# Splitting sliding-window attention into a projection phase and a core phase that runs between the steps of SSM kernel generation

## The chip, the cores and the metric

The kernel runs on one core of a Trainium2 chip. The metric is the device time of one execution in microseconds (us). Before the change the median of 15 runs was 621.43 us (620.1 to 622.94). The spread of one kernel's runs is a few us, so a difference of 3 us in a single trace is not read as an effect.

PE is the matmul engine, PEld its weight loads, DVE the vector engine, ACT the scalar engine, POOL GpSimd, SP the sync engine, which here only issues DMAs. ACTq and SPq mark DMA issues on an engine's queue.

## The reference, cut to what matters

```python
g = sigmoid((x * gate_w).sum(-1, keepdims=True))
a = attention(x)          # 32 heads of 20; each position sees 8 positions, 2 apart
b = ssm(x)                # long convolution
return g * a + (1 - g) * b

# attention: qkv = x @ wqkv ; logits = q . k[gathered] ; softmax over 8 ; sum with v ; @ wo
# ssm:       K[d, l] = Re sum_n C B dt exp(dt A l)     (192 states, 2048 steps)
#            y = irfft(rfft(x, 4096) * rfft(K, 4096)) + x * Dskip
```

S is 2048 and D is 640. Attention and the SSM kernel K do not depend on each other. Only the last line joins them.

## The kernel before

It has three stages, one after the other.

1. Attention in four blocks of 512 positions, projection and core together. The arithmetic that turns the SSM parameters into the operand tables `Sprm` is cut into steps, and `hook()` puts some steps between the parts of attention.
2. Generation of K in ten chunks. A chunk builds its arguments by matmul (`ar`), takes sines (`qtr`, `ptr`) and exponentials (`e0`, `e1`) on ACT, multiplies them on DVE (`qr`, `qi`, `pt`), and contracts them on PE into `kps`. The first FFT step of each chunk goes straight into `bufA` in SBUF.
3. The FFT convolution: the spectrum of x (`Bu`), the products with the kernel's spectrum (`Y`), the inverse (`bufA`, then `bp`), and the gated sum (`tt`, `ot`).

```python
# 1. core of attention, per block of SC = 512 positions (cut)
for e in range(5):
    prod = wk.tile([128, W, SC], BF16, name="prod")
    nc.vector.tensor_tensor(prod[:], q_broadcast, k_window, ALU.mult)
    # ... 32 matmuls into lg
hook()
# ... softmax on DVE, one Exp on ACT; attention weights spread to asb on PE and ACT
for e in range(5):
    pv = wkb.tile([128, W, SC], BF16, name="pv")
    nc.vector.tensor_tensor(pv[:], win(vc[:, e, :], 0, W, DIL, SC), asb[:], ALU.mult)
    op = ps.tile([128, SC], F32, name="op")
    for w in range(W):
        nc.tensor.matmul(op[:], ident[:], pv[:, w, :], start=(w == 0), stop=(w == W - 1))
    nc.scalar.activation(oT[:, e, :], op[:], ACT.Identity)

# 2. generation (cut)
for c in range(NCH):
    L = kg.load_L(c)                                       # 8 small DMAs from Sprm
    kps = pk.tile([128, 2, 512], F32, name="kps")
    def fin(c=c, kps=kps):
        kc = kk.tile([128, 8, 64, 2], BF16, name="kc")
        nc.vector.tensor_copy(kc[:], ...)
        fft_f1(nc, pk, ..., F1c, Bk, c, ...)               # Bk is a view of bufA
    kg.chunk(c, L, pa, kps, fin)

# 3. between the two halves of the convolution (cut)
nc.scalar.dma_start(PSI[:], ...)
for g in range(4):
    (nc.sync if g % 2 == 0 else nc.scalar).dma_start(gaF[...], ...)
    nc.sync.dma_start(omF[...], omS...)                    # omS: 1 - g, two bf16 per position
```

Of the kernel before, what the change touches and what calls it, by code (L numbers as in the profile page):

```python
# [51 lines left out]
class Attn:  # L52

    def __init__(self, ctx, tc, x, wqkv, wo, gate_w, ga_sb, omg_sb):
        self.tc, self.nc = tc, tc.nc
        nc = tc.nc
        self.x, self.ga, self.omg = x, ga_sb, omg_sb
        ind_np, ident_np, sel_np, mask0_np = _attn_consts()
        cst = ctx.enter_context(tc.tile_pool(name="at_cst", bufs=1))
        self.cst = cst  # L60
        self.wq_sb = cst.tile([128, NKT, 3 * D], BF16, name="wq_sb")
        self.xT = cst.tile([128, NKT, S], BF16, name="xT")
        self.ident = cst.tile([128, 128], BF16, name="ident")
        nc.scalar.dma_start(self.ident[:], nc.inline_tensor(ident_np, name="c_ident").ap())
        wr = wqkv.rearrange("(k p) c -> p k c", p=128)
        for kt in range(NKT):
            nc.scalar.dma_start(self.wq_sb[:, kt], wr[:, kt])
        self.ind = cst.tile([128, 32], BF16, name="ind")
        nc.scalar.dma_start(self.ind[:], nc.inline_tensor(ind_np, name="c_ind").ap())
        self.sel = cst.tile([128, 4, 128], BF16, name="sel")  # L70
        nc.scalar.dma_start(self.sel[:], nc.inline_tensor(sel_np, name="c_sel").ap())
        self.mask0 = cst.tile([128, W, 32], F32, name="mask0")
        nc.scalar.dma_start(self.mask0[:], nc.inline_tensor(mask0_np, name="c_mask0").ap())
        self.gw_sb = cst.tile([128, NKT], BF16, name="gw_sb")
        nc.scalar.dma_start(self.gw_sb[:], gate_w.rearrange("(k p) -> p k", p=128))
        self.wo_sb = cst.tile([128, 5, D], BF16, name="wo_sb")
        nc.scalar.dma_start(self.wo_sb[:], wo.rearrange("(p e) c -> p e c", e=5))
        self.g_sb = cst.tile([128, 16], F32, name="g_sb")

    def prologue(self, ctx):  # L80
        tc, nc = self.tc, self.nc
        self.wk = wk = ctx.enter_context(tc.tile_pool(name="at_wk", bufs=2))
        self.ps = ps = ctx.enter_context(tc.tile_pool(name="at_ps", bufs=2, space=PSUM))
        xT, ident = self.xT, self.ident
        xnp = tc.tile_pool(name="at_xn", bufs=1)
        xpool = xnp.__enter__()
        xn = xpool.tile([128, 16, D], BF16, name="xn")
        xr = self.x.rearrange("(i p) d -> p i d", p=128)
        for sc in range(NSC):
            nc.sync.dma_start(xn[:, 4 * sc:4 * sc + 4], xr[:, 4 * sc:4 * sc + 4])  # L90
        for sc in range(NSC):
            c0 = sc * SC
            for kt in range(NKT):
                tx = ps.tile([128, SC], F32, name="pj")
                for i in range(4):
                    nc.tensor.matmul(tx[:, i * 128:(i + 1) * 128], xn[:, 4 * sc + i, kt * 128:(kt + 1) * 128], ident[:], start=True, stop=True)
                nc.scalar.activation(xT[:, kt, c0:c0 + SC], tx[:], ACT.Identity)
            gz = ps.tile([128, SC], F32, name="pj")
            for i in range(4):
                for kt in range(NKT):  # L100
                    nc.tensor.matmul(gz[:, i:i + 1], xT[:, kt, c0 + i * 128:c0 + (i + 1) * 128], self.gw_sb[:, kt:kt + 1], start=(kt == 0), stop=(kt == NKT - 1))
            ge = wk.tile([128, 4], F32, name="ge")
            nc.scalar.activation(ge[:], gz[:, 0:4], ACT.Exp, scale=-1.0)
            nc.vector.tensor_scalar(ge[:], ge[:], 1.0, None, ALU.add)
            gs = self.g_sb[:, 4 * sc:4 * sc + 4]
            nc.vector.reciprocal(gs, ge[:])
            nc.vector.tensor_scalar(self.omg[:, 4 * sc:4 * sc + 4], gs, -1.0, 1.0, ALU.mult, ALU.add)
        xnp.__exit__(None, None, None)

    def run(self, ctx, hook=lambda: None, gaS=None):  # L110
        tc, nc = self.tc, self.nc
        wk, ps = self.wk, self.ps
        wkb = ctx.enter_context(tc.tile_pool(name="at_wkb", bufs=2))
        xT, wq_sb, ind, ident, sel = self.xT, self.wq_sb, self.ind, self.ident, self.sel
        scale = float(DH) ** -0.5
        kprev = vprev = None
        for sc in range(NSC):
            c0 = sc * SC
            qc = wk.tile([128, 5, SC], BF16, name="qc")
            kc = wk.tile([128, 5, HALO + SC], BF16, name="kc")  # L120
            vc = wk.tile([128, 5, HALO + SC], BF16, name="vc")
            if sc == 0:
                nc.vector.memset(kc[:, :, 0:HALO], 0.0)
                nc.vector.memset(vc[:, :, 0:HALO], 0.0)
            else:
                nc.vector.tensor_copy(kc[:, :, 0:HALO], kprev[:, :, SC:SC + HALO])
                nc.vector.tensor_copy(vc[:, :, 0:HALO], vprev[:, :, SC:SC + HALO])
            kprev, vprev = kc, vc
            for which, dst, off in ((0, qc, 0), (1, kc, HALO), (2, vc, HALO)):
                for e in range(5):  # L130
# [4 lines left out]
                    nc.scalar.activation(dst[:, e, off: off + SC], pp[:], ACT.Identity)  # L135
            lg = ps.tile([128, 4, W, 32], F32, name="lg", bufs=1)
            for e in range(5):
                prod = wk.tile([128, W, SC], BF16, name="prod")
                nc.vector.tensor_tensor(prod[:], qc[:, e, :].unsqueeze(1).to_broadcast([128, W, SC]), win(kc[:, e, :], 0, W, DIL, SC), ALU.mult)  # L139
                for i in range(4):  # L140
                    for w in range(W):
                        nc.tensor.matmul(lg[:, i, w, :], prod[:, w, i * 128:(i + 1) * 128], ind[:],  # L142
                                         start=(e == 0 and w == 0 and i % 2 == 0), stop=(e == 4), skip_group_check=True)
            hook()
            lgs = wk.tile([128, 4, W, 32], F32, name="lgs")
            if sc == 0:
                nc.vector.tensor_tensor(lgs[:, 0], lg[:, 0], self.mask0[:], ALU.add)
# [3 lines left out]
            mx = wk.tile([128, 4, 32], F32, name="mx")  # L151
            nc.vector.tensor_reduce(mx[:], lgs[:].rearrange("p i w h -> p i h w"), AX.X, ALU.max)
            nc.vector.tensor_tensor(lgs[:], lgs[:], mx[:].unsqueeze(2).to_broadcast([128, 4, W, 32]), ALU.subtract)
            nc.scalar.activation(lgs[:], lgs[:], ACT.Exp, scale=scale)
            sm = wk.tile([128, 4, 32], F32, name="sm")
            nc.vector.tensor_reduce(sm[:], lgs[:].rearrange("p i w h -> p i h w"), AX.X, ALU.add)
            rs = wk.tile([128, 4, 32], F32, name="rs")
            nc.vector.reciprocal(rs[:], sm[:])
            at = wkb.tile([128, 4, W, 32], BF16, name="at")
            nc.vector.tensor_tensor(at[:], lgs[:], rs[:].unsqueeze(2).to_broadcast([128, 4, W, 32]), ALU.mult)  # L160
            atT = wkb.tile([128, 2, SC], BF16, name="atT")
            for wg in range(2):
                tp = ps.tile([128, SC], F32, name="tb")
                for i in range(4):
                    nc.tensor.matmul(tp[:, i * 128:(i + 1) * 128], at[:, i, 4 * wg:4 * wg + 4, :].rearrange("p w h -> p (w h)"), ident[:], start=True, stop=True)
                nc.scalar.activation(atT[:, wg, :], tp[:], ACT.Identity)
            asb = wkb.tile([128, W, SC], BF16, name="asb", bufs=1)
            for w in range(W):
                ab = ps.tile([128, SC], F32, name="tb")
                nc.tensor.matmul(ab[:], sel[:, w % 4, :], atT[:, w // 4, :], start=True, stop=True)  # L170
                nc.scalar.activation(asb[:, w, :], ab[:], ACT.Identity)  # L171
            hook()
            oT = wkb.tile([128, 5, SC], BF16, name="oT", bufs=1)
            for e in range(5):
                pv = wkb.tile([128, W, SC], BF16, name="pv")
                nc.vector.tensor_tensor(pv[:], win(vc[:, e, :], 0, W, DIL, SC), asb[:], ALU.mult)  # L176
                op = ps.tile([128, SC], F32, name="op")
                for w in range(W):
                    nc.tensor.matmul(op[:], ident[:], pv[:, w, :], start=(w == 0), stop=(w == W - 1))  # L179
                nc.scalar.activation(oT[:, e, :], op[:], ACT.Identity)  # L180
            hook()
            for i in range(4):
                it = sc * 4 + i
                for hf in range(2):
                    ap_ = ps.tile([128, SC], F32, name="op")
                    for e in range(5):
                        nc.tensor.matmul(ap_[:, :320], oT[:, e, i * 128:(i + 1) * 128], self.wo_sb[:, e, hf * 320:(hf + 1) * 320], start=(e == 0), stop=(e == 4))
                    nc.scalar.activation(self.ga[:, it, hf * 320:(hf + 1) * 320], ap_[:, :320], ACT.Identity, scale=self.g_sb[:, it:it + 1])  # L188
            if gaS is not None:
# [515 lines left out]
```

## Time and profile before

| stage | ends at (us) | length (us) |
|---|---|---|
| 1, until the first sine eviction `qtr` on ACT | 258.0 | 258.0 |
| 2, until the last `kps` matmul | 487.1 | 229.0 |
| 3, until the end | 620.8 | 133.7 |

The next lines are the busy time by stretch of the kernel before. Behind each stretch stand its length, then for each engine the busy us and, in brackets, the number of instructions. The last three columns are PE's mean granted clock (1.00 is full), the mean busy share of the DMA engines, and GB/s.

```profile
core 0: us, PE busy (x) PEld busy (x) DVE busy (x) ACT busy (x) POOL busy (x), PEclk, DMA share, GB/s
180.00:240.00 60.00, 38.95 (x227) 18.00 (x231) 40.13 (x25) 22.01 (x38) 0.00 (x0) 0.71 0.32 63
300.00:360.00 60.00, 51.57 (x1217) 26.15 (x1219) 40.42 (x54) 58.24 (x68) 8.39 (x6) 0.50 0.08 18
...
0.00:256.00 256.00, 183.63 (x1465) 101.89 (x1484) 170.39 (x131) 122.32 (x204) 3.87 (x7) 0.89 0.24 64
261.00:486.00 225.00, 179.93 (x4026) 92.20 (x4028) 152.56 (x207) 214.42 (x249) 22.60 (x16) 0.50 0.06 14
487.00:621.00 134.00, 88.59 (x1096) 58.37 (x1088) 78.59 (x75) 61.39 (x44) 0.00 (x0) 0.79 0.37 96
```

Stage 1 leaves every engine idle for long: in its last part ACT works 22 of 60 us. Stage 2 is held by ACT, which works 58.24 of 60 us, while DVE has a third of its time free. PE is busy for 51.57 of 60 us there, with no single wait longer than 1.7 us (view of waits), but at a granted clock of 0.50. That is the opening for the change: put the idle-rich work beside the ACT-bound work.

The following line is the share of each engine in the chain of waits of the kernel before, that is, in the chain that ended last:

```profile
PE 24%; ACT 19%; DVE 11%; DMA 4%; issue 2%; ACTq 0%; SPq 0%; DVEq 0%
```

Around the turn of stage 3 the timeline of the kernel before reads as follows. Its columns are start, duration, engine, line, operation, output <- input, and in square brackets the idle time of the engine before it with the releaser.

```profile
565.02 12.04 ACTq L561 DMA_DIRECT2D gaF<-gaS  x2
565.08 12.07 SPq L562 DMA_DIRECT2D omF<-omS  x2
...
569.02 0.82 DVE L552 TENSOR_TENSOR Y<-ta,tb__8394 128x1280 bf16<-128x1280 bf16 x1
569.90 3.23 PEld L569 LDWEIGHTS <-Y 64*128 64x128 bf16 x63 [2.34 <-DVE Y L552]
...
577.11 3.65 ACT L574 ACTIVATE bufA<-bp 128x2048 bf16<-128x2048 f32 x2 [11.44 <-DMA PSI<-c_psi]
```

The bracket of the last line names the PSI load.

### The profile page before, as it was taken

The page shows a single profiled execution, that of the slowest core. Times are in us where ns is not written, and L with a number is a line of the kernel's source. Part 1 is how long each engine was busy: PE and PEld are TensorE (multiplying, and loading weights), DVE is VectorE, ACT ScalarE, POOL GpSimd, SP SyncE. Part 2 cuts the span into 40 slices and gives each one's busy share as a digit, 9 for nine tenths or more (in the row PEclk, how much of TensorE's full clock was granted, in tenths as well). Part 3 has the DMA queues.
Part 4 walks back from the last instruction along what each step waited for, and adds up shares of the span by engine and source line. Part 5 has one row for each costly group of instructions (what it writes and reads, how often), then busy time and mean ns, then how long its engine had stood idle before and what let it go on. Part 6 is the DMA issues. An engine that isn't in the chain of part 4 may idle for free.

```text
span 620.8 us, 14895 instructions
## 1 busy us (share of the span) xinstructions
PE 455.1 (73%) x6681; PEld 254.2 (41%) x6700; DVE 401.5 (65%) x413; ACT 399.2 (64%) x498; POOL 28.3 (5%) x24
## 2 busy tenths in 40 slices
PE   0749988899828469468877977977977459995562
PEld 0514644554513133234334434443434334443461
DVE  0116999799998815037767677677586654775266
ACT  0715584874614162599999999999999246773620
POOL 0000000000000000301101110110100000000000
PEclk9988999989956788755555555555555558998777
DMA  8241120110104610301000100100000320006925
GB/s 332 69 96 17 49 61 4 43 33 1 44 0 90 111 43 0 93 5 23 22 2 22 21 7 17 23 10 14 22 2 2 127 86 0 2 0 239 200 49 127
DMA packets 57430, 32.72 MB, mean 53 GB/s; under 512 B 51734, under 2 KB 56342, under 8 KB 57110
## 3 DMA queue, kind: packets, MB, share of 16 engines
q1 hardware_dynamic: 39926, 15.95, 11.0%
q10 hardware_dynamic: 17440, 15.82, 8.9%
q8 instruction: 52, 0.85, 0.6%
q14 instruction: 12, 0.10, 0.0%
HBM read 23.56 MB, written 8.20 MB: 51 GB/s over the span
## 4 chain that ended last, share of the span: by engine, by line
PE 24%; ACT 19%; DVE 11%; DMA 4%; issue 2%; ACTq 0%; SPq 0%; DVEq 0%
ACT e L405 7%; PE ar L391 5%; PE kps L439 5%; PE bp L537 5%; PE ar L397 4%; ACT qtr L403 3%; ACT ptr L403 2%; DVE pt L427 2%; DMA PSI<-c_psi 2%; DVE Bu L525 2%; ACT sp_k L542 1%; ACT sp_u L542 1%; DMA out_dram<-ot 1%; PE bp L540 1%; DVE qr L428 1%
## 5 line engine op out<-in xcount | busy, mean ns | idle before, releaser
L391 PE MATMUL ar<-Rarg,L 50*128 50x256 bf16 (+1 forms) x640 | 89.9, 373 | 40.8 <-ACT e L405 15.8
L405 ACT ACTIVATE e<-ar 128x1024 bf16<-128x1024 f32 (+1 forms) x120 | 90.7, 811 | 7.7 <-PE ar L391 4.2
L133 PE MATMUL pj<-xT,wq_sb 128*128 128x512 bf16 x286 | 75.7, 404 | 11.2 <-ACT qc L135 8.0
L403 ACT ACTIVATE qtr<-ar 128x1024 bf16<-128x1024 int16 x60 | 58.8, 1040 | 6.1 <-PE ar L391 6.0
L391 PEld LDWEIGHTS <-L 50*128 50x128 bf16 x640 | 32.6, 109 | 71.3 <-issue 51.0
L403 ACT ACTIVATE ptr<-ar 128x1024 bf16<-128x1024 int16 x60 | 59.1, 1043 | 0.3
L176 DVE TENSOR_TENSOR pv<-vc,asb 128x4096 bf16<-128x4096 bf16 x20 | 44.9, 2284 | 18.9 <-ACT asb L171 13.9
L133 PEld LDWEIGHTS <-wq_sb 128*128 128x128 bf16 x300 | 35.1, 121 | 42.8 <-issue 19.6
L439 PEld LDWEIGHTS <-pt 128*32 128x32 bf16 (+1 forms) x2560 | 33.2, 112 | 46.1 <-issue 35.0
L439 PE MATMUL kps<-qr,pt 128*32 128x64 bf16 (+1 forms) x1280 | 46.9, 236 | 4.1 <-DVE pt L427 4.1
L397 PE MATMUL ar<-Rarg,L 50*64 50x256 bf16 (+1 forms) x640 | 45.9, 388 | 5.1 <-ACT ptr L403 1.7
L179 PE MATMUL op<-pv,ident 128*128 128x512 bf16 x155 | 44.2, 434 | 7.5 <-DVE pv L176 6.2
L362 POOL MEMSET L<- 2x1536 bf16 x20 | 28.1, 1404 | 412.3 <-ACT ga L188 251.8
L139 DVE TENSOR_TENSOR prod<-qc,kc 128x4096 bf16<-128x4096 bf16 x20 | 45.5, 2285 | 0.0
L439 PE MATMUL kps<-qi,pt 128*32 128x64 bf16 (+1 forms) x1280 | 44.3, 237 | 0.3 <-DVE qi L431 0.3
L426 DVE TENSOR_SCALAR en<-e 128x1024 bf16<-128x1024 bf16 x30 | 14.0, 466 | 44.8 <-ACT e L405 44.8
L427 DVE TENSOR_TENSOR pt<-ptr,e 128x2048 bf16<-128x2048 bf16 x30 | 36.5, 1217 | 0.0
L648 DVE CAST bufA<-bp 128x1024 bf16<-128x1024 f32 x20 | 24.5, 1225 | 16.2 <-PE bp L489 16.2
L142 PE MATMUL lg<-ind,prod 128*128 128x32 bf16 x640 | 21.7, 180 | 17.2 <-DVE prod L139 15.1
L180 ACT ACTIVATE oT<-op 128x512 bf16<-128x512 f32 x20 | 11.8, 595 | 31.7 <-PE op L179 31.7
L537 PEld LDWEIGHTS <-PHI 128*128 128x128 bf16 x256 | 23.3, 101 | 20.3 <-issue 7.9
L142 PEld LDWEIGHTS <-prod 128*128 128x128 bf16 x640 | 20.3, 99 | 26.6 <-DVE prod L139 20.0
(141 smaller groups left out, 719.1 us busy)
## 6 DMA issues: line engine op xcount, KB each, us to landing
PSI<-c_psi ACTq DMA_DIRECT2D x1, 4096.0 KB, 12.6
PHI<-c_phi ACTq DMA_DIRECT2D x1, 3072.0 KB, 12.1
Sprm<-pc SPq DMA_DIRECT2D x12, 240.0 KB, 2.3
L<-Sprm SPq DMA_DIRECT2D x80, 36.0 KB, 1.8
xn<-in_A_x_dram SPq DMA_DIRECT2D x4, 640.0 KB, 11.5
gaS<-ga SPq DMA_DIRECT2D x4, 640.0 KB, 3.2
wq_sb<-in_A_wqkv_dram ACTq DMA_DIRECT2D x5, 480.0 KB, 7.1
Usb<-in_A_x_dram SPq DMA_DIRECT2D x2, 640.0 KB, 7.9
```

What stands on the lines that cost most here:

```text
L133: nc.tensor.matmul(pp[:], wq_sb[:, kt, which * D + e: (which + 1) * D: 5], xT[:, kt, c0:c0 + SC], start=(kt == 0), stop=(kt == NKT - 1))
L139: nc.vector.tensor_tensor(prod[:], qc[:, e, :].unsqueeze(1).to_broadcast([128, W, SC]), win(kc[:, e, :], 0, W, DIL, SC), ALU.mult)
L142: nc.tensor.matmul(lg[:, i, w, :], prod[:, w, i * 128:(i + 1) * 128], ind[:], start=(e == 0 and w == 0 and i % 2 == 0), stop=(e == 4), ski ...
L176: nc.vector.tensor_tensor(pv[:], win(vc[:, e, :], 0, W, DIL, SC), asb[:], ALU.mult)
L179: nc.tensor.matmul(op[:], ident[:], pv[:, w, :], start=(w == 0), stop=(w == W - 1))
L391: nc.tensor.matmul(ar[:, g2, ncol * sub:ncol * (sub + 1)], L[64 * g2:64 * g2 + KR, gp, u, sub, 0:128], R[64 * g2:64 * g2 + KR, c0:c0 + nco ...
L397: nc.tensor.matmul(ar[64 * c2:64 * c2 + 64, g2, ncol * sub:ncol * (sub + 1)], L[64 * g2:64 * g2 + KR, gp, c2, sub, 128:192], R[64 * g2:64 ...
L403: nc.scalar.activation(o, ar[:].bitcast(I16)[:, :, 0:1024:2], ACT.Sin, scale=SCL)
L405: nc.scalar.activation(o, ar[:, :, 0:2 * ncol], ACT.Exp)
L427: V.tensor_tensor(pt[:], ptr, e1.unsqueeze(2).to_broadcast([128, 32, 2, 32]), ALU.mult)
L439: nc.tensor.matmul(kps[32 * g:32 * g + 32, c2, 64 * ql:64 * ql + 64], pt[rows, 8 * g + ql, v, :], mv[rows, 8 * g + ql].rearrange("p h k -> ...
L537: nc.tensor.matmul(fp[:, fl, 0:320].rearrange("p (c x) -> p c x", x=32), PHI[:, f1, kind, :], B[:, :, 2 * f1 + ri].rearrange("p c q g -> p ...
```

## The change

The intent is to fill the ACT-bound generation with the DVE- and PE-heavy core of attention.

- `phase1` does transposes, gates and projections only, and stores q, k and v to DRAM. The parameter steps run between the projections.
- `core` becomes a generator of small steps in blocks of 256 positions. Generation calls `tick_hook` at each eviction, which advances the core by 0.68 step.
- The kernel's spectrum goes to DRAM (`BkS`) and is read back in stage 3. `Dskip` is added to `kc` in four tiny DVE adds per chunk in place of 32 matmuls in stage 3. PHI and x for stage 3 are loaded during chunk 7, on GpSimd's queue.
- PSI and half of `gaF` and of the outputs move from ACT's queue to GpSimd's. `bufA` evictions alternate between ACT and DVE. 48 small parameter loads become 6.

```diff
+    def phase1(ctx, self, g_sb, hook=lambda: None):
+        # ... transposes, gates
+        om2 = cst.tile([128, 16, 2], BF16, name="om2")
+        nc.vector.tensor_copy(om2[:], omg[:].unsqueeze(2).to_broadcast([128, 16, 2]))
+        nc.sync.dma_start(self.omS.rearrange("(i p) t -> p i t", p=128), om2[:])
         for sc in range(NSC):
+            for which, dstS, off in ((0, self.qS, 0), (1, self.kS, HALO), (2, self.vS, HALO)):
+                t = wk.tile([128, 5, SC], BF16, name="prj")          # 2 buffers
+                # ... projection matmuls, evicted by ACT into t
+                nc.sync.dma_start(dstS[:, :, off + c0:off + c0 + SC], t[:])
+                hook()
+    def core(self, ctx, g_sb):
+        C = 256
+        for sc in range(S // C):
+            # ... load qc, kc, vc from DRAM; the core as before, with yield after each piece;
+            #     all products after lg (tp, ab, op, ap_) share one PSUM bank, "tb"
 # KGen
+        for i in range(2):
+            L = cst.tile([128, 2, 2, 2, NST], BF16, name=f"L{i}")
+            for g2 in range(2):
+                nc.vector.memset(L[64 * g2:64 * g2 + 2], 1.0)
 # main
+        def tick_hook():
+            state["n"] += 1
+            while state["k"] < int(state["n"] * 0.68) and not state["done"]:
+                state["k"] += 1
+                next(core)                                           # (StopIteration cut)
         for c in range(NCH):
             ...
                 nc.vector.tensor_copy(kc[:], kps...)
+                for g in range(4):
+                    nc.vector.tensor_tensor(kc[32 * g:32 * g + 1, :, 0, :], ..., Dk[32 * g:32 * g + 1, c], ALU.add)
+                if c == 7:
+                    issue_prefetch(kc[:, 0, 0, :])                   # PHI, x (Usb): GpSimd queue
+                bk = kk.tile([128, 1, 64, 8, 4], BF16, name="bk")
-                fft_f1(nc, pk, ..., F1c, Bk, c, ...)
+                fft_f1(nc, pk, ..., F1c, bk, 0, ...)
+                nc.sync.dma_start(BkS[c], bk[:, 0])
 # fft_conv
+    for c in range(NCH):
+        (nc.sync if c % 2 == 0 else nc.gpsimd).dma_start(Bk[:, c], BkS[c])
-        nc.scalar.dma_start(PSI[:], ...)
+        nc.gpsimd.dma_start(PSI[:], ...)
-            (nc.sync if g % 2 == 0 else nc.scalar).dma_start(gaF[...], ...)
+            (nc.sync if g % 2 == 0 else nc.gpsimd).dma_start(gaF[...], ...)
-            if cb % 3 != 2:
+            if cb % 2 == 0:
```

## The prediction

> **What bounds the kernel now.** The table of busy time by stretch shows three stages with different limits.
>
> 1. 0 to 256 us: attention, with the SSM's parameter arithmetic mixed in. No engine is full: from 180 to 240 us PE is busy 39 of 60 us, DVE 40, ACT 22; they wait for one another. ACT also stands still 11.4 us near 33 us (view of waits: `qc` after the issue of `bim`), issuing 24 small parameter loads.
> 2. 261 to 486 us: generation of the SSM kernel. ACT, busy 58.2 of 60 us (300 to 360), is the limit; DVE is 40 of 60, PE's granted clock 0.50.
> 3. 486 to 621 us: FFT convolution. The chain of waits has `Bu` evictions, `sp_k`/`sp_u` evictions alternating with their matmuls, 12.5 us of PSI load, the output DMAs.
>
> **What the change does.** Stage 1 keeps only projections and parameters; the rest of attention (the core) moves under stage 2, where DVE has room. Costs from the groups of instructions by form:
>
> - New stage 1: transposes and gates, about 18 us from first data; 60 projection tiles at 1.08 us (spacing of the evictions), 65 us. DVE's parameter steps (49 us) hide beneath. I estimate generation starts at 100 us instead of 261: 161 us saved.
> - New stage 2, ACT: generation 212 us, core 61 us (`asb` 19, `ga` 17, `oT` 15.5, `atT` 5, exp 5), 19 table loads at 1.28 us = 24 us, since core exponentials fall among sines: 298 us.
> - DVE there: generation 133, `kc` and eviction copies 37, Dskip adds about 6, core 129 (`prod` 47, `pv` 47, softmax 35): 305 us.
> - [...]
>
> So DVE becomes the limit with ACT beside it: three engines 80 to 90% full, [...]with one PSUM bank for most core products. I add 40 us of blocking: 305 becomes 345 us against 225 now; 120 us are given back. The q/k/v and spectrum round trips through DRAM are almost free (DMA share there 0.07 to 0.12).
>
> - Stage 3: x, PHI and GAB come early; Dskip leaves 32 matmuls (10 us busy, partly exposed); evictions alternate better. The spectrum reload (5.2 MB) runs beside the `Bu` work; the PSI wait stays. I estimate 127 us against 134. Output, PSI and spectrum DMAs move partly from ACT's queue to GpSimd's. [...]
>
> **Prediction.** 100 + 345 + 127 = 572 us, 8 in 10 between 542 and 604 us. Faster by over 2%: 0.92; within 2%: 0.06; slower: 0.02.
>
> **What would show each step.** First `qtr` eviction on ACT at 95 to 108 us. In the merged stage DVE busy 85 to 92%, ACT 82 to 90%, length 330 to 365 us; 19 table loads there (11 in generation before); granted clock mixed, 0.5 to 0.75. Stage 3 at 120 to 132 us, with a PSI wait of about 12 us.
>
> **What would make it wrong.** PE blocked on `pv` or the single bank, so that ACT starves: stage 2 over 380 us. [...]good interleaving: near 315 us. DRAM round trips, SP's one queue delaying the `L` loads, or slow GpSimd DMAs in the tail: 5 to 15 us more.

The forecast's sum: 100 + 345 + 127 = 572 us. The 40 us of blocking are the author's estimate, with no figure behind it.

## The result and the profile after

The changed kernel takes 586.73 us (median of eight runs), against 621.43. The ratio is 0.944, with a 95% interval of 0.9424 to 0.9457. A ratio is the mean time of one kernel's fast runs over that of the other's of the same rounds, so it is not quite the ratio of the medians quoted. The change is faster by 5.6%. The predicted 572 us was 15 us too low, and the time lies inside the predicted range.

| stage | before (us) | predicted | after (us) |
|---|---|---|---|
| 1 | 258.0 | 100 | 124.7 |
| 2 | 229.0 | 345 | 326.8 |
| 3 | 133.7 | 127 | 133.8 |
| sum | 620.7 | 572 | 585.3 |

So the error of the total is the sum of +25, -18 and +7 us. The busy time by stretch of the changed kernel, one line for each stage, with the columns as above:

```profile
0.00:125.00 125.00, 79.40 (x490) 45.66 (x498) 60.84 (x67) 65.46 (x108) 6.88 (x11) 0.93 0.72 172
125.00:451.00 326.00, 279.42 (x5279) 160.12 (x5277) 276.57 (x370) 279.16 (x378) 4.77 (x5) 0.74 0.25 69
451.00:585.00 134.00, 78.61 (x1112) 60.62 (x1096) 83.24 (x81) 56.97 (x42) 14.59 (x24) 0.73 0.39 115
```

The merged stage has three engines at 85 to 86% each (276.57, 279.16 and 279.42 of 326), where the kernel before had ACT at 95% (214.42 of 225). The shares of the engines in the chain of waits of the changed kernel moved too:

```profile
PE 35%; ACT 24%; DVE 18%; DMA 13%; issue 5%; SPq 5%; POOL 0%; DVEq 0%; ACTq 0%
```

The DMA share rose from 4 to 13%, and SP's queue from 0 to 5%. Most of this is new waits at the seams of the stages. Three of them stand out.

The first is in stage 1. The timeline of the changed kernel shows PE standing for 6.81 us. It waits for ACT to evict projections, and ACT in turn waits 4.89 us for the store of `qS` to free a `prj` buffer:

```profile
47.62 2.75 PE L117 MATMUL pj<-xT,wq_sb 128*128 128x512 bf16 x12
57.19 3.15 PE L117 MATMUL pj<-xT,wq_sb 128*128 128x512 bf16 x7 [6.81 <-ACT prj L119]
...
56.54 1.57 ACT L119 ACTIVATE prj<-pj 128x512 bf16<-128x512 f32 x3 [4.89 <-DMA qS<-prj]
```

The view of DMA issues (count, KB each, us to landing) shows a tiny transfer of the changed kernel with a long landing time, which SP issued at 38.34 us, just ahead of the `qS` store at 41.69:

```profile
omS<-om SPq DMA_DIRECT2D x1, 8.0 KB, 11.7
```

The second is where stage 1 ends. After the last projection (111.1 us) it takes 13.6 us until the first sine (124.7). The timeline of the changed kernel:

```profile
111.53 1.34 DVE L368 MEMSET L<- 2x1536 bf16 x1 [5.66 <-PE pj L117]
...
113.12 13.49 SPq L387 DMA_DIRECT2D L<-Sprm  x15
...
122.77 0.58 PE L412 MATMUL ar<-Rarg,L 50*128 50x256 bf16 x3 [7.81 <-DMA L<-Sprm]
123.42 1.28 ACT L424 ACT_TABLE_LOAD   x1 [11.63 <-PE ar L412]
```

The memset of `L` waits for PE's last projection, because its memory belonged to stage 1. Then SP needs 13.49 us to issue 15 small loads, and ACT stands still for 11.63 us.

The third is at the start of stage 3. Here is a part of the chain of waits of the changed kernel (start, us, what):

```profile
455.75 1.24 DVE bk L698
456.99 0.02 issue
457.01 11.07 DMA BkS<-bk
```

And the two lines of its timeline that this wait ends in:

```profile
468.25 2.29 DVE L563 CAST Bu<-bp 128x2048 bf16<-128x2048 f32 x1 [11.27 <-DMA BkS<-bk]
468.38 1.88 ACT L563 ACTIVATE Bu<-bp 128x2048 bf16<-128x2048 f32 x1 [20.22 <-DMA BkS<-bk]
```

Both engines that could evict `Bu` wait for the store of the last spectrum chunk. `Bu` is not that chunk's data. It was given the memory of `bk`, and may not overwrite it before the store has read it.

The parts of stage 3, from the marks in the two traces, cancel almost exactly:

| part of stage 3 | before (us) | after (us) |
|---|---|---|
| last `kps` to first PHI matmul | 22.1 | 32.1 |
| first PHI matmul to end of `Y` | 60.6 | 49.0 |
| end of `Y` to first `tt` | 27.1 | 28.1 |
| first `tt` to end | 23.9 | 24.6 |

The stretch that lost the Dskip matmuls is 11.6 us shorter, about what was expected of them (10 us busy). No run undid this step alone. The wait for `bk` took 10.0 of it back.

### The profile page after: what moved, and what is told of

Its sections match the earlier page's. It is cut to its first block, busy times and chain, and to the rows that moved or that the text cites. A ratio compares the mean times of both kernels' runs of the same rounds, so it can differ in the third digit from the quotient of the medians.

```text
span 585.3 us, 15431 instructions
## 1 busy us (share of the span) xinstructions
PE 437.4 (75%) x6853; PEld 266.4 (46%) x6860; DVE 420.6 (72%) x518; ACT 401.6 (69%) x527; POOL 26.2 (4%) x40
## 4 chain that ended last, share of the span: by engine, by line
PE 35%; ACT 24%; DVE 18%; DMA 13%; issue 5%; SPq 5%; POOL 0%; DVEq 0%; ACTq 0%
PE pj L117 7%; PE tb L198 6%; ACT qtr L424 5%; ACT e L426 5%; PE ar L412 4%; ACT ptr L424 4%; PE bp L575 4%; SPq L600 4%; PE kps L460 4%; DVE prod L153 3%; PE ar L418 3%; DMA qS<-prj 3%; PE tb L208 2%; DMA xn<-in_A_x_dram 2%; DVE Bu L563 2%
## 5 line engine op out<-in xcount | busy, mean ns | idle before, releaser
L412 PE MATMUL ar<-Rarg,L 50*128 50x256 bf16 (+1 forms) x640 | 78.5, 320 | 30.8 <-DMA L<-Sprm 9.1
L117 PE MATMUL pj<-xT,wq_sb 128*128 128x512 bf16 x293 | 67.3, 386 | 9.0 <-ACT prj L119 8.4
L198 PE MATMUL tb<-pv,ident 128*128 128x256 bf16 x320 | 55.5, 330 | 2.0 <-ACT oT L199 0.8
L195 DVE TENSOR_TENSOR pv<-vc,asb 128x2048 bf16<-128x2048 bf16 x40 | 48.1, 1218 | 11.0 <-PE tb L198 7.6
L153 DVE TENSOR_TENSOR prod<-qc,kc 128x2048 bf16<-128x2048 bf16 x40 | 47.7, 1214 | 10.2 <-PE lg L156 10.1
L119 ACT ACTIVATE prj<-pj 128x512 bf16<-128x512 f32 x60 | 33.6, 594 | 17.8 <-PE pj L117 9.3
L198 PEld LDWEIGHTS <-ident 128*128 128x128 bf16 x320 | 33.9, 115 | 16.8 <-issue 5.5
L156 PE MATMUL lg<-ind,prod 128*128 128x32 bf16 x640 | 26.8, 183 | 4.8 <-DVE prod L153 3.2
L208 PE MATMUL tb<-wo_sb,oT 128*128 128x320 bf16 x160 | 28.2, 306 | 2.7 <-ACT ga L209 1.3
L199 ACT ACTIVATE oT<-tb 128x256 bf16<-128x256 f32 x40 | 15.4, 384 | 21.1 <-PE tb L198 21.0
## 6 DMA issues: line engine op xcount, KB each, us to landing
PSI<-c_psi POOLq DMA_DIRECT2D x1, 4096.0 KB, 16.6
PHI<-c_phi POOLq DMA_DIRECT2D x1, 3072.0 KB, 11.6
```

Source lines behind the costliest of these rows:

```text
L117: nc.tensor.matmul(pp[:], wq_sb[:, kt, which * D + e: (which + 1) * D: 5], xT[:, kt, c0:c0 + SC], start=(kt == 0), stop=(kt == NKT - 1))
L153: nc.vector.tensor_tensor(prod[:], qc[:, e, :].unsqueeze(1).to_broadcast([128, W, C]), win(kc[:, e, :], 0, W, DIL, C), ALU.mult)
L156: nc.tensor.matmul(lg[:, i, w, :], prod[:, w, i * 128:(i + 1) * 128], ind[:], start=(e == 0 and w == 0 and i == 0), stop=(e == 4), skip_gr ...
L195: nc.vector.tensor_tensor(pv[:], win(vc[:, e, :], 0, W, DIL, C), asb[:], ALU.mult)
L198: nc.tensor.matmul(op[:, 0, :], ident[:], pv[:, w, :], start=(w == 0), stop=(w == W - 1))
L208: nc.tensor.matmul(apf[:, :320], oT[:, e, i * 128:(i + 1) * 128], wo_sb[:, e, hf * 320:(hf + 1) * 320], start=(e == 0), stop=(e == 4))
```

## The experiments

Twelve kernels ran, all edits of the changed kernel or of each other. The theory from the prediction was that DVE limits the merged stage, with blocking on PSUM. The rival was that no single engine limits it: the chain passes from engine to engine in a fixed order. For the seams, the theories were the three waits shown above.

### Less work on one engine of the merged stage (wrong results on purpose)

```diff
 # s_dve: 16 of 40 pv products left out, about 19 us of DVE
-                pv = ...; nc.vector.tensor_tensor(pv[:], ...)
+                if e in (0, 2, 4):
+                    pv = ...; nc.vector.tensor_tensor(pv[:], ...)
 # s_act: no exponential among the sines: 8 table loads fewer, about 10 us of ACT
-            nc.scalar.activation(lgs[:], lgs[:], ACT.Exp, scale=scale)
+            nc.scalar.activation(lgs[:], lgs[:], ACT.Identity, scale=scale)
 # s_pe: half of the op matmuls
-                for w in range(W):
+                for w in range(W // 2):
```

> Wrong result on purpose: only 3 of 5 pv products per block are computed (the others' matmuls reuse an old one), which takes 16 x 1.22 = 19.5 us of DVE work out of the merged stage and leaves PE and ACT as they are. Theory 1 (DVE limits the merged stage, as predicted): the stage (first qtr eviction to last kps matmul, 327 us in the changed kernel) shrinks by 15 to 20 us. Rival (ACT or PE sets the length, DVE only follows): under 6 us. Mixed (three engines nearly full, waits handed round): 6 to 14 us.

> Wrong result on purpose: the core's softmax uses Identity in place of Exp on ACT, same size, so no table switch is needed in the middle of the sines: 8 of 19 table loads (10 us of ACT) go, nothing else changes. If ACT limits the merged stage: 8 to 10 us shorter. If DVE limits it: under 3 us.

> Wrong result on purpose: each op product sums 4 of its 8 windows, so 160 of 320 matmuls of 256 columns go, 17 us of PE array time at full clock and 34 us at half clock. If PE limits the merged stage: 15 to 30 us shorter. If it is DVE: under 4 us; the granted clock in the stage may fall[...].

| run | median (us) | ratio to before | first sine (us) | last `kps` (us) | merged stage (us) | mean clock of the run |
|---|---|---|---|---|---|---|
| changed kernel | 586.73 | 0.944 | 124.7 | 451.5 | 326.8 | 0.776 |
| s_dve | 582.41 | 0.9369 | 121.9 | 446.2 | 324.3 | 0.773 |
| s_act | 587.68 | 0.9454 | 121.4 | 452.5 | 331.1 | 0.773 |
| s_pe | 589.67 | 0.9486 | 121.8 | 454.1 | 332.3 | 0.716 |

The busy time by stretch of s_dve, then that of s_act, in the window of the changed kernel's merged stage, shows that the work was gone (DVE 263.11 against 276.57 us, ACT 267.85 against 279.16; s_act has 11 table loads in the merged stage, of 1283 ns each, and the changed kernel 19):

```profile
125.00:451.00 326.00, 280.62 (x5338) 160.96 (x5335) 263.11 (x361) 278.17 (x377) 6.92 (x9) 0.71 0.25 72
```

```profile
125.00:451.00 326.00, 283.88 (x5183) 161.50 (x5181) 278.16 (x370) 267.85 (x369) 4.77 (x5) 0.72 0.24 69
```

In e_bk, e_om, e_actq, e_prj and e_oms (below), which leave the work of this stage as it is but for one small store in e_oms, the stage took 326.1 to 329.3 us, so 3 us are its spread. Taking 19 us from DVE brought 4 us in the total, but only 2.5 us of it in the stage itself, within that spread; the rest is that generation began 2.8 us earlier, which the edit does not touch. Taking 10 us from ACT brought nothing, and taking half of the `op` matmuls from PE brought nothing or a small loss. A limit would have paid back most of what was taken from it. So DVE was not the limit that the prediction named, and ACT alone is not the limit either. For PE the run does not decide, because PE's clock changed with it.

The run s_pe shows that PE stayed as busy. First the busy time by stretch of the changed kernel, then that of s_pe:

```profile
125.00:225.00 100.00, 86.35 (x1586) 50.92 (x1586) 89.36 (x116) 89.45 (x120) 0.00 (x0) 0.71 0.22 64
225.00:325.00 100.00, 88.45 (x1660) 51.10 (x1652) 91.59 (x122) 83.96 (x117) 0.00 (x0) 0.79 0.20 59
```

```profile
125.00:225.00 100.00, 85.89 (x1513) 46.26 (x1510) 90.76 (x117) 86.96 (x116) 0.00 (x0) 0.62 0.21 61
225.00:325.00 100.00, 90.41 (x1572) 47.34 (x1571) 88.83 (x118) 84.08 (x117) 0.00 (x0) 0.64 0.20 60
```

And one group of instructions by form in the merged stage, the `op` matmuls, again of the changed kernel first. The columns are the count, busy us and mean ns of one, and the idle time before them with its releasers.

```profile
L198 PE MATMUL tb<-pv,ident 128*128 128x256 bf16 x320 | 55.5, 330 | 2.0 <-ACT oT L199 0.8 <-DVE pv L195 0.7
```

```profile
L198 PE MATMUL tb<-pv,ident 128*128 128x256 bf16 x160 | 41.4, 413 | 1.0 <-DVE pv L195 0.5
```

Half as many matmuls, but PE was busy as long as before. The granted clock fell from 0.71 and 0.79 to 0.62 and 0.64, and each remaining matmul took 413 ns instead of 330. So in this run less PE work came with less clock; what sets the clock, no run shows. (The 17 and 34 us of the expectation fit the changed kernel's trace: eight `op` matmuls take 1.05 us from 158.92 us on, at a granted clock of 1.00, and 1.89 us from 151.41 us on, at 0.50. A single one takes 0.27 and 0.40 us, so it is about 0.11 or 0.21 us for each further one, and 18 or 34 us for 160.) The group also bears on the prediction's fear about the single PSUM bank: before these matmuls PE waited for the bank's eviction (`oT`) for 0.8 us in the whole stage. It was ACT that waited for the matmuls, for 21.0 us in all (view of waits). No run gave the core a second bank, so whether that would shorten these waits is not shown.

```diff
 # s_all: the three edits together
```

> Wrong result on purpose: the three cuts s_dve, s_act and s_pe at once (DVE 19.5 us, ACT 10 us, half of the op matmuls). Each alone changed the merged stage by +5 to -5 us. Theory 1 (three engines limit by turns: what one is relieved of, another holds up): together they shorten it by 15 us or more. Theory 2 (the order of instructions, fixed when the program is built, and the hand-overs in the core's chain set the pace, not the amount of work): under 8 us.

The three together took 580.09 us (ratio 0.9344), and the last `kps` came at 443.2 us. The merged stage was 322.1 us long, against 326.8. Cutting DVE by about 19 us, ACT by 10 and half of the `op` matmuls at once shortened it by 4.7 us, and PE's clock fell again. Its busy time by stretch:

```profile
125.00:225.00 100.00, 90.92 (x1526) 47.17 (x1526) 84.91 (x112) 85.67 (x118) 0.00 (x0) 0.59 0.22 63
225.00:325.00 100.00, 91.93 (x1665) 47.82 (x1664) 87.73 (x118) 83.34 (x115) 0.00 (x0) 0.64 0.21 61
```

DVE and ACT are less busy here, and PE is busier, at a clock of 0.59 and 0.64. In the whole run's chain of waits PE has 40%, against 35%. The result lies in the range of theory 2 (under 8 us), but it does not prove it: PE, slower and busier, may have been what held the stage here. That PE's clock hands back much of what is saved fits both runs without half of the `op` matmuls. What the stage would take at a constant clock, no run could show.

### The core not interleaved

```diff
 # e_serial
-        kg.hook = tick_hook
+        kg.hook = lambda: None
```

> Correct result: the split stays, but the attention core is not interleaved; it runs after the generation. Generation alone should take 225 us as in the kernel before (ACT-bound), the core alone 130 to 170 us (DVE's 129 us and its waits). If the gain comes from overlap of the two, as predicted, this kernel is 30 to 70 us slower than the merged one, 615 to 655 us, and not faster than before. If the gain came mostly from the cheaper loads and tail, it stays near 590 us.

This run was correct and took 656.65 us, a ratio of 1.056 (1.053 to 1.059). All the rest of the change was in it. So without the interleaving the split is 5.6% slower than the kernel before, and the interleaving itself is worth 70 us (656.65 minus 586.73), at the upper end of what was expected. Its busy time by stretch shows the clock falling back:

```profile
121.00:384.00 263.00, 226.73 (x4621) 118.65 (x4622) 210.84 (x303) 230.09 (x281) 4.80 (x6) 0.51 0.25 69
384.00:530.00 146.00, 93.14 (x705) 58.95 (x704) 73.17 (x75) 45.89 (x90) 2.64 (x5) 0.72 0.20 68
```

Without most of the core's matmuls among its own, generation runs at a clock of 0.51, much as before the change (0.50). The separation is not clean: generation's stretch still holds 210.84 us of DVE work, more than the 152.56 of the kernel before, so some of the core still ran beside it (23 of the 40 `prod` and 10 of the 40 `pv` products). That may also be why generation took 262 us (121.1 to 383.4) and not the expected 225. The 70 us are therefore the difference between this little interleaving and the full one; a kernel with no overlap at all was not run.

### The seam to stage 3

```diff
 # e_bk: bk in a pool of its own, on the other side of SBUF
+        bkp = c2.enter_context(tc.tile_pool(name="bkp", bufs=2, side="right"))
-                bk = kk.tile([128, 1, 64, 8, 4], BF16, name="bk")
+                bk = bkp.tile([128, 1, 64, 8, 4], BF16, name="bk")
```

> Correct result: the spectrum tile bk moves to a pool of its own, elsewhere in SBUF. Theory: after the generation the first Bu evictions stand still 11 us (DVE) and 20 us (ACT), since Bu was laid over bk, whose last store must drain behind 4.7 MB of reload on the same queues. Then 9 to 11 us faster than the changed kernel (about 576 us). Rival: the reload itself is what stage 3 waits for; then the wait only moves to the first spectrum matmul, and under 3 us are gained.

It was correct, with 578.33 us and a ratio of 0.9307 (0.9281 to 0.9332), 8.4 us less than the changed kernel. The wait is gone. In the timeline of e_bk, DVE begins to evict `Bu` 1.10 us after the issue of the last store begins:

```profile
456.72 0.32 SPq L700 DMA_DIRECT2D BkS<-bk  x1
...
457.82 2.29 DVE L563 CAST Bu<-bp 128x2048 bf16<-128x2048 f32 x1 [1.14 <-PE bp L510]
```

Stage 3 was 124.5 us long instead of 133.8. So the wait was one for memory, not for data. (In the changed kernel this last store took 11.1 us to land, against a median of 2.8 us of the ten, and SP had issued four loads of the reload since 451.55 us. That it drained behind them, as the theory has it, would fit; no run isolates it.) Its removal gave 8.4 us in the total and 9.3 us in the stage, a little less than the 11.07 us in the chain and the 9 to 11 us expected.

### The turn of the convolution

```diff
 # e_om: the four small omF loads ahead of the four gaF loads
 # e_actq: the same, and PSI and half of gaF back on ACT's queue
-        nc.gpsimd.dma_start(PSI[:], ...)
+        nc.scalar.dma_start(PSI[:], ...)
-            (nc.sync if g % 2 == 0 else nc.gpsimd).dma_start(gaF[...], ...)
+            (nc.sync if g % 2 == 0 else nc.scalar).dma_start(gaF[...], ...)
```

> Correct result: the four small omF loads are issued before the four gaF loads. Theory: the tail's first multiply waits 7.6 us for omF only because it stands behind gaF in SP's queue, where one issue took 12.7 us. Then 6 to 8 us faster (about 579 us). Rival: gaF or the inverse transform is next at once: under 3 us.

> Correct result: as e_om (omF first), but PSI and half of gaF are issued from ACT's queue, as in the kernel before. Theory: what the profile before calls a wait for PSI is ACT standing 12 us in the issue of gaF, behind which its bufA evictions queue; then ACT's first bufA eviction is 8 to 11 us later than in e_om and the kernel 5 to 9 us slower than e_om. Rival (my prediction's reading: the data of PSI is waited for whoever issues it): e_actq equals e_om within 2 us.

In the timeline of the changed kernel `tt` waits for `omF`, whose issues stand behind large `gaF` loads on SP's queue:

```profile
533.31 12.70 SPq L600 DMA_DIRECT2D omF<-omS  x1
...
534.54 1.88 ACT L612 ACTIVATE bufA<-bp 128x2048 bf16<-128x2048 f32 x1 [6.15 <-PE bp L607]
...
560.74 1.49 DVE L624 TENSOR_TENSOR tt<-bp,omF 128x1280 bf16<-128x1280 f32 x1 [7.56 <-DMA omF<-omS]
```

With `omF` first (e_om, 583.88 us, ratio 0.9412) the first `tt` came at 552.3 us instead of 560.7. The total fell by only 2.9 us: the part after the first `tt` grew from 24.6 to 28.7 us, and a new wait of `ot` for `gaF` (3.4 us) shows in it. Part of the gain was only passed on to the next load, as the rival had it. The intervals of the two ratios overlap (0.9378 to 0.9446 against 0.9424 to 0.9457), so the gain in the total is not clear of noise; the earlier `tt` is.

The run e_actq settles what held ACT in the kernel before. It took 595.53 us (ratio 0.9592), 11.7 us more than e_om, more than the 5 to 9 us expected. ACT's first `bufA` eviction came 16.1 us later than in e_om (532.58 us). ACT's timeline in e_actq:

```profile
533.43 14.78 ACTq L601 DMA_DIRECT2D gaF<-gaS  x2
548.65 3.65 ACT L613 ACTIVATE bufA<-bp 128x2048 bf16<-128x2048 f32 x2 [19.86 <-DMA omF<-omS]
```

The bracket now names `omF`, which the eviction does not read, and in the kernel before it named PSI, which it does not read either. In both, ACT begins to evict within half a microsecond of the end of the issues (577.06 and 548.21 us). With these loads on GpSimd's queue, ACT evicts at 534.54 us. So the wait of 11.4 us in the kernel before was the issuing, and the change took it away. (The two `gaF` loads that ACT issued took 19.9 us, median, to land in the kernel before and 17.0 us in e_actq.)

### The seams of stage 1

```diff
 # e_prj: four buffers for the projections
-                t = wk.tile([128, 5, SC], BF16, name="prj")
+                t = wk.tile([128, 5, SC], BF16, name="prj", bufs=4)
```

> Correct result: the projection output tile has 4 buffers instead of 2. Theory: in stage 1 ACT waits 4.9 and 3.3 us and PE 6.8 us because a tile can't be reused until its DRAM store has drained (first store 14.7 us). Then generation starts 7 to 10 us earlier and the kernel is 6 to 10 us faster (about 578 us). Rival: the DMA engines are the limit there (share 0.97 from 40 to 60 us), and the wait moves to the Sprm stores and L loads: under 3 us.

It brought nothing: 588.46 us, ratio 0.9468. The projections ended at 114.9 us (111.1 before the edit), and between 30 and 125 us ACT now waited 13.8 us for stores of `Sprm` (4.2 before the edit), as the rival had it. The missing buffer was not the cause, only the place where it showed. The next suspect was the store of `omS`, 2048 pieces of 4 bytes, issued just ahead.

```diff
 # e_oms: the store of omS moved to chunk 1 of generation (om2 kept in a longer-lived pool)
+                if c == 1:
+                    nc.vector.scalar_tensor_tensor(om2[:], kc[:, 0, 0:16, :], 0.0, om2[:], ALU.mult, ALU.add)
+                    nc.sync.dma_start(omS.rearrange("(i p) t -> p i t", p=128), om2[:])
```

> Correct result: the store of omS (2048 elements of 4 bytes, which took 11.7 us from issue to landing at 38 us) is moved out of stage 1 into the merged stage. Theory: it, and not the number of buffers, is what clogged the DMA engines there (share over 1.1 at 20 to 50 GB/s from 40 to 48 us), so that the first projection store landed after 14.7 us and PE waited 6.8 us; e_prj only moved that wait to the Sprm stores. Then the projections end 6 to 9 us earlier (102 to 105 us instead of 111), generation starts 5 to 9 us earlier, and the kernel is 5 to 9 us faster (about 579 us). Rival: the bytes of q, k, v and Sprm are the limit; under 2 us.

The DVE instruction only ties the store to chunk 1, so that it is not issued earlier. The run was correct, with 577.97 us and a ratio of 0.929 (0.9249 to 0.9332), 8.8 us less. The projections ended at 102.9 us. Here is the busy time of two stretches of 2 us of the changed kernel, then of the same two of e_oms:

```profile
44.00:46.00 2.00, 2.00 (x11) 1.12 (x10) 0.00 (x0) 1.13 (x2) 0.00 (x0) 1.00 1.42 40
46.00:48.00 2.00, 2.00 (x11) 1.07 (x10) 0.00 (x0) 0.60 (x1) 0.00 (x0) 1.00 1.23 32
```

```profile
44.00:46.00 2.00, 2.00 (x11) 1.09 (x10) 0.91 (x1) 1.19 (x2) 0.00 (x0) 1.00 1.03 334
46.00:48.00 2.00, 2.00 (x11) 1.11 (x10) 0.00 (x0) 1.35 (x3) 0.00 (x0) 1.00 1.07 341
```

The DMA engines are full in both (share above 1), but with `omS` among the transfers they move 32 to 40 GB/s, without it 334 to 341. Eight kilobytes in pieces of 4 bytes held up 640 KB of projections. In the kernel before this store took 11.0 us too, but nothing waited for it.

### All repairs together

```diff
 # combo: e_bk + e_om + e_oms, and
 #  - L tiles in a long-lived pool, their memsets at the start; half of the first chunk's L loads on ACT's queue
 #  - gate_w loaded ahead of the later x blocks
 #  - x for stage 3 (Usb) loaded one quarter each in chunks 2 to 5 instead of all in chunk 7
 # combo2: combo, and
 #  - Rarg (constant operand of ar) loaded at the start
 #  - core advanced by 0.61 step per tick instead of 0.68
```

> Correct result, meant to beat both: bk in its own pool (e_bk: 8 us), omF first (e_om: about 3 us), omS later (e_oms: 5 to 9 us if the theory holds), gate weights loaded before the rest of x (about 5 us idle of PE there), the first two L tiles laid where they need not wait for stage 1's memory and half of the first one's loads on ACT's queue (3 to 6 us), and the prefetch of x for the FFT in four parts over four chunks instead of at once. Sum 20 to 30 us: 557 to 567 us. In each run with the whole prefetch at once PE stood 2 to 5 us with nothing to wait for while it ran; if that is due to the burst of small packets, the gap is gone here; if it is something in the program at that place, it stays.

> Correct result: combo with two more edits that act in different stages. (a) The constant Rarg is loaded at the start: in combo generation waited for it (issued at 100.2 us, used at 108.9), so it should start 4 to 7 us earlier than 110.8. (b) The core is spread over the whole generation (0.61 of a step per tick instead of 0.68), so that the last chunks, where PE, DVE and ACT are busy only 65 to 75%, get work too. If spreading helps, the merged stage (327.7 us in combo) falls to 318 to 323 us; if the pace is a sum of hand-overs, it stays within 3 us. Time 549 to 558 us.

Both were correct. combo took 561.37 us (ratio 0.9042, 0.9011 to 0.9072), combo2 558.27 us (0.8983, 0.8952 to 0.9013). combo2 beats the changed kernel by 4.9% (558.27 over 586.73). The three single repairs gained 8.4, 2.9 and 8.8 us, 20.1 in sum. combo gained 25.4, so its other edits are worth about 5 us, if the gains simply add up.

In combo the first sine still came 13.6 us after the last projection (97.2 to 110.8 us). With `L` there earlier, another load had become the last one. This is combo's timeline:

```profile
100.24 0.36 ACTq L369 DMA_DIRECT2D Rarg<-c_rarg  x1
...
108.85 1.03 PE L404 MATMUL ar<-Rarg,L 50*128 50x256 bf16 x8 [8.22 <-DMA Rarg<-c_rarg]
```

combo2 loads `Rarg` at the start, and its first sine came at 104.6 us, 5.7 us after the last projection. The merged stage stayed as long as it was: 327.7 us in combo and 329.4 in combo2. Spreading the core further did not help it. combo2's time lies just above the 549 to 558 us expected.

One small effect stayed argued. In the changed kernel, while `Usb` was loaded in chunk 7, PE stood still with no wait that the profile knows. Its timeline:

```profile
424.83 0.21 PE L460 MATMUL kps<-qr,pt 64*32 64x64 bf16 x8
430.10 0.25 PE L460 MATMUL kps<-qi,pt 64*32 64x64 bf16 x8 [5.06 <-issue]
```

In combo and combo2, with the load split into four, no gap of this size is there. In e_bk, e_om, e_oms, e_actq and s_dve, with the whole load at once, PE has 4.2 to 5.1 us of such idle time at this line. What it stood for is not shown: the profile names no wait, and no run changed this load alone. Nor are the small packets of the expectation shown: from 420 to 432 us the queue q0 moved 295 packets with 1.07 MB in the changed kernel, 3.6 KB on average (view of DMA queues).

## Why the prediction was right or wrong

**Direction and size.** Faster by over 2% was right. The forecast gain was 50 us, and 35 came. The mechanism was right in its main lines: 133 us less in stage 1, and 98 us given back in stage 2. It was wrong in what limits the merged stage (below). That the total was off by only 15 us is partly luck: +25 and +7 us stand against -18, and the -18 of stage 2 is itself the sum of -28 and +10 (below).

**Stage 1, predicted 100, measured 124.7.** This is the term that was mis-sized, by 25 us. "60 projection tiles at 1.08 us (spacing of the evictions), 65 us" took 75 to 77 us, because the `omS` store held up the projection stores; in e_oms, without that store, they took 65.4 us (first to last eviction, 37.6 to 103.0 us), as forecast. The other 13 us lie between the last projection and the first sine, where the prediction had no term at all. They were waits for the `L` memory and loads, and behind them for `Rarg`. The prediction did name "SP's one queue delaying the `L` loads" as a danger, at 5 to 15 us together with other DMA troubles.

**Stage 2, predicted 345, measured 326.8.** The prediction added the durations of instructions: 305 us for DVE and 298 for ACT. Added up over the groups of the trace after, they are 299 and 300 us, so the inventory was within 2%. But the engines are busy for only 277 and 279 us, because the instructions of one engine overlap. Two sines, of 1.02 to 1.04 us when one stands alone, occupy 1.94 us together in the timeline of the changed kernel:

```profile
204.17 1.94 ACT L424 ACTIVATE qtr<-ar 128x1024 bf16<-128x1024 int16 x2
```

They overlap by 0.10 to 0.14 us (2 times 1.02 minus 1.94, and 2 times 1.04 minus 1.94). So 305 should have been 277. The blocking was put at 40 us and came to 50 (327 minus 277). "So DVE becomes the limit" was wrong: 19 us less of DVE gained 4 us in all and 2.5 us in this stage. That "one PSUM bank for most core products" blocks PE does not show in the waits (0.8 us before the `op` matmuls), but no run tried a second bank. The table loads were 19 as forecast, at 1283 ns each. DVE was busy for 85% and ACT for 86%, at the low end and in the middle of what was forecast. The clock was mixed, where 0.5 to 0.75 had been forecast: 0.74 on average, 0.69 to 0.83 in stretches of 50 us and 0.52 in the last 26 us. The stage's length was just under the 330 to 365 us that were named as the sign.

**Stage 3, predicted 127, measured 133.8.** The gain expected from Dskip fits the stretch that got 11.6 us shorter, though no run isolates it. The term that was missing is the wait for `bk`'s memory, 9 us by e_bk. "The PSI wait stays" was a misreading: it was ACT issuing `gaF`, and the change removed it. What was won was lost again to `omF` in SP's queue (7.6 us).

**GpSimd's queue.** The prediction named slow GpSimd DMAs as a danger. No run isolates their speed. PHI landed in 11.6 us from GpSimd's queue, and in 12.1 us from ACT's before; but PSI took 16.6 us against 12.6, and the four parts of `Usb`, issued together with PHI, 20.5 us (median) against 7.9 and 10.4. The transfers beside them changed too, so the cause is not shown.

**What stays open.** What order of steps would make the merged stage shorter than 322 to 332 us, and how long it would be at a constant PE clock, was not settled. Three rivals stand untested against each other: PE at its granted clock, the single PSUM bank, and the fixed order in which the engines hand work to each other. In the changed kernel three engines were busy for about 85% and the chain passed between them.

## What to carry to other kernels

When you move a stage's work under another stage, cost the seams as well as the work: memory handed from one stage to the next, the last small load before the new stage's first instruction, small loads queued behind large ones, and large stores behind a tiny one in very small pieces (8 KB in pieces of 4 bytes, 11.7 us to land). Here three such seams (`bk`, `omF`, `omS`) cost about 20 us by single repairs, more than the whole error of the forecast (15 us), and repairing all the seams gained 4.9% while the merged stage stayed as long as it was. When three engines are 85% busy in a fixed order, do not look for the limit by busy share; take work from one engine and see what the stage gives back, and look at PE's clock when you do: here it fell from 0.71 and 0.79 to 0.62 and 0.64 with half of the `op` matmuls. And where a bracket names a DMA whose data the instruction does not read, look whether the engine was issuing DMAs at that time, as ACT was here for 12.04 and 14.78 us.
